# A PSUM bank for each group of the first transform, and odd rows tile by tile in turns

## The chip, the cores and the metric

The kernel runs on one core of a Trainium2 chip. The metric is the time of one execution on the device in microseconds (us). The engines of the core work beside each other, each through its own list of instructions in order: TensorE (PE, matrix products; PEld is its weight load), VectorE (DVE), ScalarE (ACT), GpSimd (POOL) and SyncE (SP), which here only issues DMAs. They wait for each other and for DMAs by semaphores. PE writes its products to PSUM, which has eight banks; DVE and ACT read them there.

## The reference

```python
x: (8, 3008, 256)                       # 8 sequences of 3008 rows
X = np.fft.fft(x, axis=1)
X = np.fft.fft(X, axis=2)
a = X.real.astype(np.float32).reshape(8 * 3008, 256)
h = a @ w_in                            # 256 -> 2048
r = np.maximum(h, 0.0)
out = (r * r) @ w_out                   # 2048 -> 256
```

All of it is float32.

## The kernel before

A two-dimensional Fourier transform whose real part is kept splits into cosine and sine products. For each sequence the kernel forms two tables in SBUF, P (`Pt`, from cosines along the rows) and Q (`Qt`, from sines), and a single row E (`Et`) for the middle column of the 256. E is the work of one row; in the first sequence it is carried through PE in the last, else unused, row of Q's products. Behind the transform follow the two layers: `front` multiplies P and Q with w_in, which has been multiplied with the second transform's tables (`G1`, `G2`), DVE joins the results (L637 to L640), ACT does relu and square (`combine`), and `back` multiplies with w_out. The output columns go in 6 blocks of up to 251, and each block in 8 steps `j` over the hidden dimension; `steps` is that list over all sequences.

The transforms of sequences 1 to 7 run spread between the steps of the sequence before (`between`). The transform of sequence 0 has nothing to hide behind: it is the prologue, and its order is written out by hand, in `pieces`, `groups` and the calls from `start()` to `spread_rest()`. The schedule is manual: on each engine the instructions stand in the order in which the program names them.

The prologue's parts are these.

- Seven row tiles of x are loaded (`load_x`). Tiles 0 to 3 belong to even rows (classes 0, 1, 2), tiles 4 to 6 to odd rows (class 3; `ODD0` is 4). `for_p(t)` folds tile t for P on DVE (L379, L395, L409) and ACT puts E's column into `lone` (L412, shown as `wsum`, whose memory it borrows; all its other columns are zero). `for_q(t)` folds it for Q (L383, L399, L409).
- Tables: `cosT` and `sinT`, loaded by SP (L183), first the cosines, then the odd tiles' sines, then win 1, then the even tiles' sines, then win 2 and further weights (L237).
- For P and for Q, and in each for two parities kp of the output column, there is a `group` of operations. `even_n` forms the even rows' products (L488) into one bank and ACT copies a part of them (`da`, L506). `join_4` and `join_2` combine the classes on DVE (L520/L524 for P, L515/L517 for Q). `odd_n` forms the odd rows' products. `join_1` combines both into `Pt`; for Q it comes as `join_lo` and `join_hi`.
- E: `even_e` and `odd_e` write E's products with `lone` (`wsum`) into a bank first, row 127 of the results, and Q's `even_n` and `odd_n` then add Q's 127 rows in the same banks.
- `begin_win(j)` starts to convert a part of w_in: two DVE operations split the number (L252, L257), ACT does three (L254, L255, L259), and `rounded(j)` the rest on DVE (L262, L264, L265). `win[j][1]` multiplies it with the second transform's tables (L280) and ACT copies the result to `G1`, `G2` (L281). `win[j][2]` forms one column for E (L289), and what it returns copies that to `gE` (L291).
- `awake(n)` issues n products of the identity matrix whose result nobody reads.
- `spread_e` spreads E's first 251 values over the partitions (L612, ACT L613); `spread_rest` does the rest through DRAM.

PSUM is shared out in three pools. `psd`, tag d, has two banks; `psh`, tag h, has two (the banks of `front`'s `ph`); `psm` has one bank each for mA, mB, mC, mD (the accumulators of `back`; mC and mD also take the products of L280). In the prologue before the change: `filled` (of `awake`) sits in mB; even rows of P take the two banks of d, one for each parity; even rows of E and Q take the same two banks after them; odd rows of P take the two h banks; odd rows of E and Q take mA for kp 0 and an h bank for kp 1; L289 of j = 0 takes mC, and `spread_e` a bank of d.

The numbers in `groups_at` count the list of operations: 0 to 4 are P's for kp 0 (even_n, join_4, join_2, odd_n, join_1), 5 to 9 the same for kp 1, 10 to 17 are Q's for kp 0 (even_n, join_4, join_2, odd_n, join_lo, even_e, odd_e, join_hi), and 18 to 25 those for kp 1.

Of the kernel before, what the change touches and what calls it, by code (L numbers as in the profile page):

```python
# [8 lines left out]
F32 = mybir.dt.float32  # L9
# [4 lines left out]
P = 128  # L14
# [68 lines left out]
def kernel(  # L83
# [13 lines left out]
    B, NROW, _, D = x.shape  # L97
# [7 lines left out]
    CH = 256  # L105
# [3 lines left out]
    NT = len(TILES)  # L109
# [16 lines left out]
    psh = ctx.enter_context(tc.tile_pool(name="psh", bufs=2, space=PSUM))  # L126
    psd = ctx.enter_context(tc.tile_pool(name="psd", bufs=2, space=PSUM))
    psm = ctx.enter_context(tc.tile_pool(name="psm", bufs=1, space=PSUM))
# [9 lines left out]
    ODD0 = NT - 3  # L138
# [60 lines left out]
    nc.vector.memset(ramp[:, 1:2], 255.0 * 2.0 ** 23)  # L199


    filled = psm.tile([P, CH], F32, name="filled", tag="mB")

    def awake(n):
        for _ in range(n):
            nc.tensor.matmul(filled[:, 0:P], ident, ident, start=True, stop=True)


    def pair_in(j):

        return moe_w_in.rearrange("(c p) (h j f) -> j c p h f", p=P, j=NJ, h=2)[j]
# [5 lines left out]
    def parts(w, k):  # L217
        return w.rearrange("p c (e h) -> p h (c e)", h=k)
# [22 lines left out]
    def convert(dst, raw):  # L241


        k = dst.shape[1]
        if raw.dtype == F32:
            return lambda: nc.vector.tensor_copy(dst, parts(raw[:, :, :, 0], k))
        low, high = raw[:, :, :, 0], raw[:, :, :, 1]
        m = scratch()
        e = fp.tile([P, 2, CH], F32, name="fd", tag="fd")
        mb, eb, rest = m.bitcast(U32), e.bitcast(U32), low.bitcast(F32)  # L250

        nc.vector.tensor_scalar(out=eb, in0=high, scalar1=20, scalar2=0x7FF,  # L252
                                op0=ALU.logical_shift_right, op1=ALU.bitwise_and)
        act(e, eb, AF.Relu, bias=ramp[:, 0:1], scale=-1.0)  # L254
        act(eb, e, AF.Relu, bias=ramp[:, 1:2], scale=-2.0 ** 23)  # L255

        nc.vector.tensor_scalar(out=mb, in0=high, scalar1=0xFFFFF, scalar2=0x100000,  # L257
                                op0=ALU.bitwise_and, op1=ALU.bitwise_or)
        act(rest, low, AF.Copy, scale=2.0 ** -32)  # L259

        def finish():
            nc.vector.scalar_tensor_tensor(out=eb, in0=high, scalar=0x80000000, in1=eb,  # L262
                                           op0=ALU.bitwise_and, op1=ALU.bitwise_or)
            tt(out=m, in0=mb, in1=rest, op=ALU.add)  # L264
            nc.vector.scalar_tensor_tensor(out=dst, in0=parts(m, k), scalar=2.0 ** -20, in1=parts(e, k),  # L265
                                           op0=ALU.mult, op1=ALU.mult)

        return finish


    def begin_win(j):

        w = ep.tile([P, 2, CH], F32, name="win", tag="sB" if j % 2 else "sA")
        finish = convert(parts(w, 1), win.pop(j, None) or load(pair_in(j)))

        def products():
            for tab, G, nm in ((cosd, G1, "mC"), (sind, G2, "mD")):
                pg = psm.tile([P, CH], F32, name="pg", tag=nm)
                for i in range(2):
                    nc.tensor.matmul(pg, tab[:, i], w[:, i], start=i == 0, stop=i == 1)  # L280
                nc.scalar.copy(G.rearrange("p (h j f) -> j p h f", h=2, j=NJ)[j],  # L281
                               pg.rearrange("p (h f) -> p h f", h=2))

        def for_e():

            ps = psd.tile([P, CH], F32, name="pe", tag="d") if j else psm.tile([P, CH], F32, name="pe", tag="mC")
            for h in range(2):
                fc = j + NJ * h
                nc.tensor.matmul(ps[:, h:h + 1], G2[:, fc * P:(fc + 1) * P], last, start=True, stop=True)  # L289

            return lambda: nc.vector.tensor_scalar_mul(gE[:, j::NJ], ps[:, 0:2], 0.5)  # L291

        win[j] = finish, products, for_e
# [42 lines left out]
    def columns(tab, t, part):  # L336

        nk, at = NC[0][3], PLACE[t]
        nq = (nk + 1) // 2
        return tab[:, 0, at + part * nq:at + (nk if part else nq)]  # L340
# [120 lines left out]
    def dft_ops(b):  # L461
# [7 lines left out]
        def group(kp, which):  # L469
            both_in = b == 0 and which == 1  # L470
            n = NE if b is None else P - 1 if which == 1 and b else P
            tab = sinT if which == 1 else cosT
            n2, _, n1, n0 = NC[kp]
            st = {}

            def product(ps, c, lone_e=False):

                ts = [t for t in range(NT) if TILES[t][0] == c]
                for t in ts:
                    rows = TILES[t][3]  # L480
                    if b is None:
                        w = we[0:rows, kp, t, 0:n]
                    elif lone_e:
                        w = lone[0:rows, 2 * t + kp]
                    else:
                        w = folded[b, t][0:rows, kp, PART[which]]
                        w = w if which else w[:, 0:n]
                    nc.tensor.matmul(ps[0:w.shape[-1]], w,  # L488
                                     (cosT if lone_e else tab)[0:rows, kp, PLACE[t]:PLACE[t] + NC[kp][c]],
                                     start=t == ts[0] and (lone_e or not both_in), stop=t == ts[-1] and not lone_e,  # L490
                                     skip_group_check=both_in)

            EVEN = ((0, 0, n2), (1, n2, n2), (2, 2 * n2, n1))

            def even_e():
                st["ps"] = psd.tile([P, 512], F32, name="pd", tag="d")
                for c, at, nk in EVEN:
                    product(st["ps"][:, at:at + nk], c, True)

# [33 lines left out]
                st["c"] = hp.tile([P, NC[0][3]], F32, name="dc2", tag="dc2", bufs=2)[0:n, 0:n0]  # L533
                both(st["c"][:, 0:n1], st["c"][:, n1:n0], a, ps[:, 2 * n2:2 * n2 + n1])

            def odd_tile():

                pool, tag = (psd, "d") if b != 0 else (psm, "mA") if kp == 0 and both_in else (psh, "h")
                ps = pool.tile([P, 512], F32, name="pd", tag=tag)[0:n]
                st["odd"] = ps[:, 0:n0]  # L540
                return ps

            def odd_e():
                product(odd_tile()[:, 0:n0], 3, True)

            def odd_n():
                if both_in:
                    return product(st["odd"], 3)
                ps = odd_tile()
                if not b:  # L550
                    return product(ps[:, 0:n0], 3)
                nq = (n0 + 2) // 2 if kp else (n0 + 1) // 2
                for part in range(2):
                    if kp:
                        tab, o = (cosT, sinT)[part], 0
                        to = ps[:, part * nq:part * nq + nq]
                        other = part != which
                    else:
                        tab, o = (cosT, sinT)[which], part
                        to = ps[:, part:n0:2]  # L560
                        other = part != which
                    for i, pair in enumerate(((ODD0, ODD0 + 1), (ODD0 + 2, NT))):
                        nc.tensor.matmul(to, folded[b, pair[other]][:, kp, PART[which]][:, 0:n],  # L563
                                         columns(tab, ODD0 + i, o), start=i == 0, stop=i == 1)
                if kp:
                    st["cos"] = hp.tile([P, nq], F32, name="oc", tag="oc", bufs=1)[0:n]
                    nc.scalar.copy(st["cos"], ps[:, 0:nq])
                    st["sin"] = ps[:, nq:2 * nq]
# [21 lines left out]
                both(dst[:, kp:kp + 2 * n0 - 1:2], dst[:, M - kp - 2 * (nh - 1):M - kp + 1:2], st["c"],  # L590
                     st["odd"], only)

            if both_in:
                return [(0.0, f) for f in (even_n, join_4, join_2, odd_n, join_lo, even_e, odd_e, join_hi)]
            ops = [(0.1, even_n), (0.4, join_4), (0.5, join_2), (0.1, odd_n), (0.8, join_1)]
            if b and kp:
                ops.insert(4, (0.5, join_odd))
# [179 lines left out]


    pieces = [fold(0, t) for t in range(NT)]
    start, *groups = [f for _, f in dft_ops(0)]  # L780

    def for_p(t):
        for i in (0, 2, 4):
            pieces[t][i]()

    def for_q(t):
        for i in (1, 3, 5):
            pieces[t][i]()

    def groups_at(*which):  # L790
        for i in which:
            groups[i]()

    def rounded(j):
        win[j][0]()
# [26 lines left out]
    win[0][1]()  # L822
    awake(2)
    for_p(3)
    groups_at(0, 5, 15, 23)
    for_q(1)
    for_p(4)
    for_p(5)
    for_q(2)
    for_p(6)  # L830
    groups_at(3, 8, 1, 2)
    for_q(4)
    groups_at(6, 7)
    for_q(5)
    groups_at(4, 16, 24)
    for_q(6)
    groups_at(13, 21, 9)
    copy_e = win[0][2]()
    begin_win(1)
    for_q(3)  # L840
    groups_at(10, 18)
    awake(14)
    rounded(1)
    begin_win(2)
    groups_at(11, 12, 14, 19, 20, 22)
    spread_e()
    groups_at(17, 25)
    copy_e()
    spread_rest()
    LAG = 2  # L850
# [39 lines left out]
    for i in range(len(steps) + LAG + 4):  # L890
        if i < len(steps):
            b, k0, n, j = steps[i]
# [96 lines left out]
```

## Time and profile before

| what | us |
|---|---|
| median of 5 runs (1949.26 to 1951.45) | 1949.78 |
| the profiled execution | 1949.47 |
| its span, first to last instruction | 1947.5 |
| PE busy (99% of the span) | 1933.3 |
| DVE busy (72%) | 1395.0 |
| ACT busy (47%) | 924.8 |
| POOL busy (60%) | 1173.8 |
| start of L612, the first product behind the prologue | 47.67 |

A line of the timeline gives start, length, engine, line, operation, out<-in, the shapes and the number of instructions; in brackets stands the idle time before it and what ended that. An f32 product is two records on PE. The chain that ended last is the work followed back from the end, at each step to what released it. PEclk, or "clock" in a table by stretches, is the TensorE clock that was granted, as a part of full speed; it was 0.996 in the mean.

### The profile page before, as it was taken

Reading aid. Unit: us, or ns where it says so; the run is one execution under the profiler, and the core shown is the slowest. Engines: PE = TensorE matmul, PEld = TensorE weight load, DVE = VectorE, ACT = ScalarE, POOL = GpSimd, SP = SyncE. Lnnn points to the kernel's source line nnn. Section 1 sums busy time; section 2 is a strip of 40 time slices with the busy share of each in tenths; the row PEclk is TensorE's granted clock in tenths of the full one; section 3 lists DMA queues with packets and bytes.
Section 4 is the critical chain, followed back from the end, with each engine's and each line's share of the span. In section 5 each row is a group of like instructions: output and inputs, shape, how many; then the busy total and the mean of one; then the engine's idle time right before and its main releaser. Section 6 shows DMA issues by size and latency. Waiting matters only on the chain.

```text
span 1947.5 us, 27716 instructions
## 1 busy us (share of the span) xinstructions
PE 1933.3 (99%) x9258; PEld 1718.9 (88%) x9258; DVE 1395.0 (72%) x3432; ACT 924.8 (47%) x1074; POOL 1173.8 (60%) x1708
## 2 busy tenths in 40 slices
PE   8999999999999999999999999999999999999998
PEld 7888888888988899888998889888898888988887
DVE  7998866777677766777667776677767777655554
ACT  2755544454444444544444454444544454444443
POOL 0047646676567665767566665666756676566655
PEclk8999999999999999999999999999999999999999
DMA  7342102111111101111011200121002101100101
GB/s 210 111 45 52 36 9 51 33 28 30 26 32 41 38 12 27 41 37 31 12 35 39 44 19 12 39 50 28 20 15 53 33 12 22 27 12 11 22 11 22
DMA packets 145562, 69.53 MB, mean 36 GB/s; under 512 B 129090, under 2 KB 136204, under 8 KB 145419
## 3 DMA queue, kind: packets, MB, share of 16 engines
q1 hardware_dynamic: 144960, 66.86, 15.9%
q8 instruction: 72, 1.18, 0.3%
q14 instruction: 71, 0.58, 0.1%
q0 software_dynamic: 176, 0.65, 0.1%
q10 hardware_dynamic: 283, 0.26, 0.0%
HBM read 43.03 MB, written 24.69 MB: 35 GB/s over the span
## 4 chain that ended last, share of the span: by engine, by line
PE 96%; DVE 3%; issue 0%; DMA 0%; ACT 0%; DVEq 0%
PE ph L635 16%; PE mC L687 16%; PE ph L634 16%; PE mA L687 16%; PE mB L687 16%; PE mD L687 8%; PE pd L488 3%; PE pd L563 2%; DVE m L264 0%; DVE fd L262 0%; DVE he L637 0%; PE mA L674 0%; PE mB L674 0%; DVE g L640 0%; DVE w L409 0%
## 5 line engine op out<-in xcount | busy, mean ns | idle before, releaser
L649 ACT ACTIVATE g<-g 128x1004 f32<-128x1004 f32 (+1 forms) x384 | 399.4, 1040 | 792.5 <-DVE g L640 459.1
L637 DVE SCALAR_TENSOR_TENSOR he<-Et,gE,ph 128x251 f32<-128x251 f32 (+1 forms) x768 | 362.1, 471 | 413.5 <-PE ph L635 411.2
L657 POOL TENSOR_TENSOR s<-g 128x251 f32<-128x251 f32 (+1 forms) x376 | 246.3, 655 | 658.8 <-ACT g L650 596.1
L634 PE MATMUL ph<-Pt,G 128*128 128x251 f32 (+1 forms) x1536 | 452.1, 375 | 0.0
L635 PE MATMUL ph<-Qt,G 127*128 127x251 f32 (+1 forms) x1536 | 451.8, 375 | 0.0
L650 ACT ACTIVATE g<-g 128x1004 f32<-128x1004 f32 (+1 forms) x384 | 399.3, 1040 | 12.1
L687 PE MATMUL mC<-s,wsum 128*128 128x251 f32 (+1 forms) x1504 | 381.7, 375 | 0.0
L687 PE MATMUL mA<-g,wout 128*128 128x251 f32 (+1 forms) x1504 | 379.8, 374 | 0.0
L639 DVE TENSOR_TENSOR g<-he,ph 128x251 f32<-128x251 f32 (+1 forms) x768 | 320.6, 417 | 55.3 <-POOL s L657 1.4
L635 PEld LDWEIGHTS ph<-Qt,G 127*128 127x128 f32 x1536 | 291.7, 190 | 36.1
L634 PEld LDWEIGHTS ph<-Pt,G 128*128 128x128 f32 x1536 | 288.0, 189 | 35.3 <-DVE g L640 0.8
L687 PEld LDWEIGHTS mC<-s,wsum 128*128 128x128 f32 x1504 | 285.7, 190 | 34.7
L687 PEld LDWEIGHTS mA<-g,wout 128*128 128x128 f32 x1504 | 282.9, 189 | 36.0 <-issue 1.3
L640 DVE TENSOR_TENSOR g<-he,ph 128x251 f32<-128x251 f32 (+1 forms) x768 | 314.3, 409 | 0.0
L659 POOL TENSOR_TENSOR s<-g 128x251 f32<-128x251 f32 (+1 forms) x376 | 305.5, 812 | 0.0
L658 POOL TENSOR_TENSOR s<-s,g 128x251 f32<-128x251 f32 (+1 forms) x376 | 274.5, 730 | 29.5
L660 POOL TENSOR_TENSOR s<-g,s 128x251 f32<-128x251 f32 (+1 forms) x376 | 253.7, 675 | 0.0
L687 PE MATMUL mB<-g,wsum 128*128 128x251 f32 (+1 forms) x752 | 220.5, 374 | 0.0
L687 PE MATMUL mD<-s,wout 128*128 128x251 f32 (+1 forms) x752 | 220.4, 374 | 0.0
L687 PE MATMUL mB<-s,wout 128*128 128x251 f32 (+1 forms) x752 | 219.9, 374 | 0.0
L687 PEld LDWEIGHTS mB<-g,wsum 128*128 128x128 f32 x752 | 142.6, 190 | 17.4
L687 PEld LDWEIGHTS mD<-s,wout 128*128 128x128 f32 x752 | 141.9, 189 | 17.7
(136 smaller groups left out, 1306.3 us busy)
## 6 DMA issues: line engine op xcount, KB each, us to landing
out_dram<-os SPq DMA_DIRECT2D x376, 56.0 KB
xt<-in_x_dram SPq DMA_DIRECT2D x32, 384.0 KB
xt<-in_x_dram SPq DMA_DIRECT2D x42, 128.0 KB
Et<-e_dram SPq DMA_DIRECT2D x7, 752.5 KB
xt<-in_x_dram SPq DMA_DIRECT2D x9, 512.0 KB
out_dram<-os SPq DMA_DIRECT2D x288, 6.8 KB
raw<-in_moe_w_in_dram SPq DMA_DIRECT2D x16, 256.0 KB
raw<-in_moe_w_out_dram SPq DMA_DIRECT2D x16, 256.0 KB
```

Of the source, the lines that this page charges most:

```text
L634: nc.tensor.matmul(hP, G1[:, fs], pt[:, ks], start=True, stop=True)
L635: nc.tensor.matmul(hQ, G2[0:P - 1, fs], qt[0:P - 1, ks], start=True, stop=True)
L637: nc.vector.scalar_tensor_tensor(out=t, in0=et[:, ks], scalar=gE[:, fc:fc + 1], in1=hP, op0=ALU.mult, op1=ALU.add)
L639: tt(out=g[:, h, 0, 0:n], in0=t, in1=hQ, op=ALU.add)
L640: tt(out=g[:, h, 1, 0:n][:, ::-1], in0=t, in1=hQ, op=ALU.subtract)
L649: act(v, v, AF.Relu)
L650: act(v, v, AF.Square)
L657: gt(out=s1, in0=g21, in1=g22, op=ALU.add)
L658: gt(out=s2, in0=s1, in1=g11, op=ALU.subtract)
L659: gt(out=s3, in0=g11, in1=g21, op=ALU.subtract)
L660: gt(out=s4, in0=g12, in1=s2, op=ALU.subtract)
L687: nc.tensor.matmul(acc[nm][:, i, 0:n], w, v[:, 0:n], start=j == 0 and i == 0, stop=j == NJ - 1, skip_group_check=True)
```

## The change

Only the prologue changes; the steps behind it are the same list of instructions on each engine.

- Banks. E's and Q's even rows get mC (kp 0) and mD (kp 1) instead of the two banks of d after P. E's and Q's odd rows get mA and mB. `filled` is taken from the two banks of d at each call of `awake`, and so is the tile of L289 for j = 0.
- The products of odd rows: instead of three tiles of one group after the other (P kp 0, P kp 1, E kp 0, E kp 1, Q kp 0, Q kp 1), the order is tile 4 of P for both parities, tile 4 of E for both, then tiles 5 and 6 in the same way, and behind them tile 4 of Q for both parities, tile 5, tile 6.
- DVE: the fold of tile 6 for Q comes ahead of P's two `join_1`, which stood on both sides of it.
- The second `awake` has 12 products instead of 14.

The diff, cut to its core; the renaming of group numbers to names is left out where the order stays.

```diff
-    filled = psm.tile([P, CH], F32, name="filled", tag="mB")
-
     def awake(n):
+        filled = psd.tile([P, CH], F32, name="filled", tag="d")
         for _ in range(n):
             nc.tensor.matmul(filled[:, 0:P], ident, ident, start=True, stop=True)
...
-            ps = psd.tile([P, CH], F32, name="pe", tag="d") if j else psm.tile([P, CH], F32, name="pe", tag="mC")
+            ps = psd.tile([P, CH], F32, name="pe", tag="d")
...
-            def product(ps, c, lone_e=False):
+            def product(ps, c, lone_e=False, only=None):
                 ts = [t for t in range(NT) if TILES[t][0] == c]
-                for t in ts:
+                for t in ts if only is None else ts[only:only + 1]:
...
             def even_e():
-                st["ps"] = psd.tile([P, 512], F32, name="pd", tag="d")
+                st["ps"] = psm.tile([P, 512], F32, name="pd", tag=("mC", "mD")[kp])
...
-            def odd_tile():
-                pool, tag = (psd, "d") if b != 0 else (psm, "mA") if kp == 0 and both_in else (psh, "h")
-                ps = pool.tile([P, 512], F32, name="pd", tag=tag)[0:n]
+            def odd_part(i, lone_e):
+                if i == 0 and lone_e == both_in:
+                    pool, tag = (psm, ("mA", "mB")[kp]) if both_in else (psh, "h")
+                    st["odd"] = pool.tile([P, 512], F32, name="pd", tag=tag)[:, 0:n0]
+                product(st["odd"], 3, lone_e, i)
...
     for_p(3)
-    groups_at(0, 5, 15, 23)
+    p_part("even")
+    q_part("even_e")
     for_q(1)
     for_p(4)
     for_p(5)
     for_q(2)
     for_p(6)
-    groups_at(3, 8, 1, 2)
+    for i in range(NT - ODD0):
+        p_part(f"odd{i}")
+        q_part(f"odd_e{i}")
+    groups[0, 0, "join_4"]()
+    groups[0, 0, "join_2"]()
     for_q(4)
-    groups_at(6, 7)
+    groups[0, 1, "join_4"]()
+    groups[0, 1, "join_2"]()
     for_q(5)
-    groups_at(4, 16, 24)
     for_q(6)
-    groups_at(13, 21, 9)
+    p_part("join_1")
+    q_part(*(f"odd{i}" for i in range(NT - ODD0)))
     copy_e = win[0][2]()
     begin_win(1)
     for_q(3)
-    groups_at(10, 18)
-    awake(14)
+    q_part("even")
+    awake(12)
     rounded(1)
     begin_win(2)
-    groups_at(11, 12, 14, 19, 20, 22)
+    for kp in range(2):
+        for nm in ("join_4", "join_2", "lo"):
+            groups[1, kp, nm]()
     spread_e()
-    groups_at(17, 25)
+    q_part("hi")
     copy_e()
```

`p_part(name)` and `q_part(name)` call the named operation of P or of Q for kp 0 and then for kp 1.

More of the change, by code (lines that the diff above doesn't have):

```diff
@@ L534, in join_2, with odd_n @@
                 both(st["c"][:, 0:n1], st["c"][:, n1:n0], a, ps[:, 2 * n2:2 * n2 + n1])
-            def odd_tile():
-                pool, tag = (psd, "d") if b != 0 else (psm, "mA") if kp == 0 and both_in else (psh, "h")
-                ps = pool.tile([P, 512], F32, name="pd", tag=tag)[0:n]
-                st["odd"] = ps[:, 0:n0]
[L541 to L550, printed above, removed]
+            def odd_part(i, lone_e):
[3 more added lines that the diff above has]
+                product(st["odd"], 3, lone_e, i)
+            def odd_n():
+                ps = psd.tile([P, 512], F32, name="pd", tag="d")[0:n]
+                st["odd"] = ps[:, 0:n0]
+                if b is None:
                     return product(ps[:, 0:n0], 3)
@@ L591, in join_1 @@
                      st["odd"], only)
-            if both_in:
-                return [(0.0, f) for f in (even_n, join_4, join_2, odd_n, join_lo, even_e, odd_e, join_hi)]
+            if b == 0:
+                named = [("even", even_n), ("join_4", join_4), ("join_2", join_2), ("lo", join_lo), ("hi", join_hi),
+                         ("join_1", join_1), ("even_e", even_e)]
+                for i in range(NT - ODD0):
+                    named += [(("odd", "odd_e")[e] + str(i), lambda i=i, e=e: odd_part(i, e == 1)) for e in range(2)]
+                return [((which, kp, nm), f) for nm, f in named]
             ops = [(0.1, even_n), (0.4, join_4), (0.5, join_2), (0.1, odd_n), (0.8, join_1)]
@@ L779 @@
     pieces = [fold(0, t) for t in range(NT)]
-    start, *groups = [f for _, f in dft_ops(0)]
+    (_, start), *groups = dft_ops(0)
+    groups = dict(groups)
     def for_p(t):
@@ L788, in for_q, with p_part, q_part @@
             pieces[t][i]()
-    def groups_at(*which):
-        for i in which:
-            groups[i]()
+    def p_part(*names):
+        for nm in names:
+            for kp in range(2):
+                groups[0, kp, nm]()
+    def q_part(*names):
+        for nm in names:
+            for kp in range(2):
+                groups[1, kp, nm]()
     def rounded(j):
@@ L830 @@
     for_p(6)
-    groups_at(3, 8, 1, 2)
+    for i in range(NT - ODD0):
+        p_part(f"odd{i}")
+        q_part(f"odd_e{i}")
+    groups[0, 0, "join_4"]()
+    groups[0, 0, "join_2"]()
     for_q(4)
-    groups_at(6, 7)
+    groups[0, 1, "join_4"]()
+    groups[0, 1, "join_2"]()
     for_q(5)
-    groups_at(4, 16, 24)
     for_q(6)
-    groups_at(13, 21, 9)
+    p_part("join_1")
+    q_part(*(f"odd{i}" for i in range(NT - ODD0)))
     copy_e = win[0][2]()
@@ L840 @@
     for_q(3)
-    groups_at(10, 18)
-    awake(14)
+    q_part("even")
+    awake(12)
     rounded(1)
     begin_win(2)
-    groups_at(11, 12, 14, 19, 20, 22)
+    for kp in range(2):
+        for nm in ("join_4", "join_2", "lo"):
+            groups[1, kp, nm]()
     spread_e()
-    groups_at(17, 25)
+    q_part("hi")
     copy_e()
```

## The prediction

> **What bounds the kernel now.** I read the page first: TensorE (PE) holds 96% of the chain that ended last and is busy 99% of the span, so only PE's idle time and its slow stretches can be won. The list of waits, PE alone, says where the idle time is:
>
> ```profile
> engine line waited for: us in total, times, longest us
> PE pd L488 <- DVE dc L524: 4.2, 1, 4.2
> PE pe L289 <- ACT G L281: 2.7, 2, 2.3
> ...
> PE mA L674 <- DVE wout L265: 0.5, 1, 0.5
> ```
>
> All of it lies before 100 us. So I read PE's timeline there (start, length, line, out<-in, number of records; a product is two records):
>
> ```profile
> 17.31 2.89 PE L488 MATMUL pd<-cosT,w 95*128 95x95 f32 x16
> 24.36 5.00 PE L488 MATMUL pd<-cosT,wsum 95*128 95x95 f32 x16 [4.16 <-DVE dc L524]
> 29.16 5.11 PE L488 MATMUL pd<-cosT,w 128*128 128x377 f32 x12
> 34.11 3.97 PE L488 MATMUL pd<-cosT,wsum 128*128 128x377 f32 x12
> 37.91 3.97 PE L488 MATMUL pd<-sinT,w 128*127 128x377 f32 x12
> 41.72 0.50 PE L289 MATMUL pe<-ident,G 128*128 128x1 f32 x4
> 42.08 2.42 PE L488 MATMUL pd<-sinT,w 95*127 95x95 f32 x16
> 44.34 3.29 PE L206 MATMUL filled<-ident 128*128 128x128 f32 x28
> 47.67 0.66 PE L612 MATMUL pe<-Qt,ident 128*128 128x251 f32 x2
> ```
>
> The reader sees E's even rows wait 4.16 us for P's joins on VectorE (DVE), which free their bank, and then take 5.00 us where the equal group at 42.08 takes 2.42. The table by stretches gives the reason, the granted clock (PE busy, clock, DMA share, GB/s):
>
> ```profile
> 17.80:21.20 3.40, 2.29 (x13) 1.00 1.02 280
> 21.20:24.60 3.40, 0.24 (x1) 0.50 1.08 296
> 24.60:28.00 3.40, 3.30 (x13) 0.50 1.05 262
> 28.00:31.40 3.40, 3.40 (x9) 0.50 0.49 96
> ...
> 55.40:58.80 3.40, 1.15 (x7) 1.00 0.00 0
> 58.80:62.20 3.40, 3.40 (x11) 0.50 0.48 154
> ```
>
> Half clock follows stretches in which PE was busy 2.29 and 1.15 of 3.4 us, and holds 10.2 us the first time. Last, the chain in order of time: from 49.27 it is DVE's nearly alone, until PE takes over for good:
>
> ```profile
> 49.27 0.49 DVE he L637
> ...
> 98.96 0.70 DVE wout L265
> 99.70 0.69 PE mA L674 x2
> ```
>
> So what counts is when step 0's first DVE operation starts (49.27). Behind 99.70 PE has no wait but 0.5 us in the last store, and a shift reaches the end whole.
>
> **The change, part by part.** *E's even rows get banks mC and mD.* Their last users, two ACT copies of G, end by 17.4, so the 4.16 us go: these products start at about 20.1, where P's even rows end. PE is then busy on through 17.8 to 21.2, with gaps of about 0.3 us; the stretches at 41.7 and 51.9, as full, kept clock 1.00, so I expect no drop at 21.2. The group then takes 2.26 (42.08 to 44.34) and not 4.80 (24.36 to 29.16), and ends at 22.4.
>
> *Odd rows of P and E in turns.* The same 36 records, each with its own weight load before and after. At full clock twelve take 3.80 (34.11 to 37.91), the first twelve took 4.95; so the odd rows end at 22.4+3x3.80 = 33.8, not 41.72: 8.0 us earlier (4.16 wait, 2.54 and 1.15 clock, 0.1 rounding). The turns let PE start with what is there. The trace holds each transfer's landing: the three odd cosine tiles land at 21.3, 22.6, 24.3 and are wanted at 22.4, 24.9, 27.4; the odd sine tiles at 26.2, 28.1, 29.7, wanted at 30.0, 31.2, 32.5. DVE's folds for them end at 23.2 (P) and, below, 29.9 (Q). Nothing stalls; the price of the turns is nil, covered by these 0.5 to 4 us.
>
> *Even rows of Q.* L289 takes 0.36, so they could start at 34.1. Their last sine piece lands at 35.04: the first parity's last tile runs 35.1 to 35.4, the second parity ends at 36.5. About 1 us of the 8.0 is lost here.
>
> *DVE's queue.* Tile 6's Q fold (1.58, from 33.33) moves ahead of P's first join, into the 4.05 us that DVE idles before 32.41: 28.3 to 29.9. P's odd rows end on PE at 28.7, so both joins (0.92 each, L520 and L524) run to 31.7; the next win's two splitting operations (0.67; its data landed at 31.0) to 32.4, tile 3's fold (1.57) to 34.0, the rounding (1.93) to 35.9. Next stand two operations on win 2, whose second half lands at 36.60. DVE is strictly in order here, so Q's joins, queued behind, wait too: they start at 36.65+0.67 = 37.3. ACT's copy for them is ready 0.63 after the last tile's second record (43.09 to 43.72 now), at 35.9, so the transfer is last. Now they start at 43.72: 6.4 us gained. SP issues the same list in the same order; a load there waits for the landing eight places before it, and buffer releases come no later, so I leave the landings where they are.
>
> *Smaller parts.* Filling matmuls 14 to 12: 12x0.224 (3.13/14, 44.34 to 47.47) = 2.7, so PE ends at 39.2; L612 needs Q's low joins, 3.95 after their start (43.72 to 47.67), at 41.25. That leaves a new idle of 2.05 us. L289's tile, the filling and L612 now share two banks; L612 gets the filling's bank, not the one that L291 still has to read, so no wait is added. P's odd rows take the ph banks, free until step 0.
>
> *The new idle and the clock.* The nearest rows are 1.15 busy of 3.4 (drop) and gaps of 0.3 to 0.5 (none). The drops and rises in the table stand 3.4 apart on one grid; where that falls in another run isn't known. If the idle falls inside one stretch, L612 and step 0's eight records run at half speed: the first L635 is 0.85 later, the second 1.7 more, of which DVE's 1.17 per half hides part: 1.4, with L612 1.8. Bounds 0 to 1.8; I take 0.8. The Trainium skill, "TensorE: Matmul & The Clock Gate", section "HAM oscillation", warns of idle gaps above some 3.4 us only; by it the sum would be 6.4 without the 0.8 (1943.4), but in this trace 2.25 us was enough.
>
> Sum: -6.4+0.8 = -5.6. From step 0 on DVE's work is unchanged up to 99.70, where PE had waited 0.54 for it. PE's own chain follows, since its wait at 58.61 is set by DVE and ACT; the half clock at 58.8 may move, but costs PE 1.7 off the chain. The profiled run took 1949.47 (span 1947.5 and 2.0 around it), so 1943.9; the median is 0.3 above it: **1944.2 us**.
>
> **The rivals.** *A, the cover is thinner.* The gain is capped by data (win 2 later by 2 to 3 us), or the clock still drops at 21.2 and holds two stretches of 3.4, moving PE 3.4 later and the joins to 39.3. For it: DMA share is 1.0 until 28 us. Against: the landings follow from one list. Gain 2 to 3.9: 1945.9 to 1947.8.
>
> *B, slower.* One mechanism: the gate does not see products in turns as busy and holds half clock from 21.2 through the P and E turns. Even rows left over cost 1.1 more, 24 odd records 7.6 more, the twelve of Q 0 to 3.8: odd rows end at 42.5 to 46.3. It decides once PE loses over 8.0 us, since then the joins start after 43.72: +0.8 to +4.6, 1950.6 to 1954.4. For it: 24.6 to 28.0, all with the mostly zero wsum, was busy 3.30 and kept 0.50. Against: 34.11 to 37.91, twelve wsum records, ran at 1.00. The same skill page, section "A second HAM failure mode: psum-queue depth-cycling", speaks against this change: cycling banks can make the gate swing; it would give these times. In this trace the rows from 64.26 on (L674) swap banks mA and mB product by product at clock 1.00, so the measurement stands against it.
>
> *C, it does nothing:* the banks are still taken and the 4.16 us appear under another name. Against: mC and mD are free at 17.4. 1949.8.
>
> **How the numbers follow.** Forecast 78% (1942.5 to 1945.9), A 14%, C 3%, B 5%. The lower bound: win 2 landing earlier frees the joins at 36.6 (-7.1) with no clock loss, 1942.7, less 0.2 of scatter. The upper: half of A, 1946.8. 0.2% (3.9 us) is what a measurement can tell here. Faster is the forecast, 0.78; same A and C, 0.17; slower B, 0.05.
>
> **What would show it.** In the changed profile: no wait at wsum products; clock 1.00 from 21 to 38; L289 near 33.8; Q's joins (L515) start near 37.3, behind win 2's L251; L612 near 41.3 with about 2 us idle before it; half clock behind that or not; first L637 42.9 to 44.3. Wrong: L515 started by ACT or PE, or a clock of 0.5 inside the turns.

## The result and the profile after

The changed kernel takes 1944.71 us in the median of 25 runs (1943.31 to 1950.0), against 1950.15 in 45 runs (1949.06 to 1951.69) of the kernel before. The ratio is 0.9977 with a 95% interval of 0.9971 to 0.9982, or 3.5 to 5.7 us less. One thing stands out beside the gain: the runs before lie within 2.6 us, those after within 6.7.

The profiled execution of the changed kernel took 1947.47, more than its median, so it shows how the slower executions come about. Its list of waits, PE alone:

```profile
engine line waited for: us in total, times, longest us
PE pd L487 <- DMA cosT<-in_cos_s_dram: 3.3, 1, 3.3
PE pe L288 <- ACT G L280: 2.7, 2, 2.2
...
PE pe L612 <- DVE Qt L515: 0.5, 1, 0.5
```

The 4.2 us for P's joins are gone. A wait of 3.3 us stands in the list that was not there before: the same products of even rows (L487, L488 before) now wait for cosine tiles. PE's timeline of that execution shows where:

```profile
16.19 0.58 PE L487 MATMUL pd<-cosT,w 95*128 95x95 f32 x4
20.05 3.71 PE L487 MATMUL pd<-cosT,w 96*128 96x189 f32 x12 [3.28 <-DMA cosT<-in_cos_s_dram]
23.55 4.43 PE L487 MATMUL pd<-cosT,wsum 95*128 95x95 f32 x16
27.77 2.10 PE L487 MATMUL pd<-cosT,w 128*128 128x377 f32 x4
29.71 1.43 PE L487 MATMUL pd<-cosT,wsum 128*128 128x377 f32 x4
...
39.83 0.50 PE L288 MATMUL pe<-ident,G 128*128 128x1 f32 x4
...
45.78 0.66 PE L612 MATMUL pe<-Qt,ident 128*128 128x251 f32 x2 [0.49 <-DVE Qt L515]
```

The wait is inside P's even rows, between class 1 and class 2, whose last transfer landed at 20.4 us here and at 18.4 in the profile before. E's even rows follow P's without a pause, as the new banks allow, but take 4.43 us and not the 2.3 that they need at full clock. The table by stretches (PE busy, clock, DMA share, GB/s) says why:

```profile
17.80:21.20 3.40, 1.15 (x4) 0.66 0.99 253
21.20:24.60 3.40, 3.40 (x15) 0.50 1.07 266
24.60:28.00 3.40, 3.40 (x13) 0.50 1.09 267
28.00:31.40 3.40, 3.40 (x10) 0.84 0.93 207
```

The clock fell at 18.9 us and stayed at 0.50 for 10.2 us. L612, the first product behind the prologue, starts at 45.78 instead of 47.67: of 8.0 us on PE 1.9 are left in this execution. From L612 to the end of the span it is 1899.9 us here and 1899.8 before, so all that the change does is done by then. Q's joins start late, and ACT's copy of PE's products releases them, not win 2:

```profile
41.84 0.32 DVE L515 SCALAR_TENSOR_TENSOR db<-pd,signs,da 128x95 f32<-128x95 f32 x1 [0.74 <-ACT da L506]
```

### The profile page after: what moved, and what is told of

Same layout as the page of the kernel before. It is cut to its first block, busy times and chain, and to the rows that moved or that the text cites. A ratio compares the mean times of both kernels' runs of the same rounds, so it can differ in the third digit from the quotient of the medians.

```text
span 1945.7 us, 27713 instructions
## 1 busy us (share of the span) xinstructions
PE 1931.1 (99%) x9254; PEld 1717.4 (88%) x9254; DVE 1394.9 (72%) x3432; ACT 924.9 (48%) x1074; POOL 1174.3 (60%) x1708
## 3 DMA queue, kind: packets, MB, share of 16 engines
q8 instruction: 72, 1.18, 0.3%
## 4 chain that ended last, share of the span: by engine, by line
PE 96%; DVE 3%; DMA 1%; issue 0%; SPq 0%; ACT 0%; DVEq 0%
PE ph L635 16%; PE ph L634 16%; PE mC L687 16%; PE mA L687 16%; PE mB L687 16%; PE mD L687 8%; PE pd L487 3%; PE pd L559 2%; DMA xt<-in_x_dram 0%; DVE m L263 0%; DVE fd L261 0%; DMA cosT<-in_cos_s_dram 0%; DVE he L637 0%; PE mA L674 0%; PE mB L674 0%
## 5 line engine op out<-in xcount | busy, mean ns | idle before, releaser
L637 DVE SCALAR_TENSOR_TENSOR he<-Et,gE,ph 128x251 f32<-128x251 f32 (+1 forms) x768 | 362.1, 472 | 413.8 <-PE ph L635 411.4
```

The lines of the kernel that those rows point to most:

```text
L637: nc.vector.scalar_tensor_tensor(out=t, in0=et[:, ks], scalar=gE[:, fc:fc + 1], in1=hP, op0=ALU.mult, op1=ALU.add)
```

## The experiments

Each kernel ran beside the kernel before. Ratios are to that.

| kernel | median us | lowest to highest | runs | ratio (95%) |
|---|---|---|---|---|
| changed kernel again | 1946.58 | 1943.94 to 1947.71 | 10 | 0.9977 (0.9968 to 0.9986) |
| banks alone | 1943.89 | 1943.23 to 1947.85 | 6 | 0.9969 (0.9958 to 0.9981) |
| turns alone | 1950.46 | 1949.39 to 1951.29 | 11 | 0.9999 (0.999 to 1.0008) |
| class 2 cosines issued first | 1946.24 | 1944.37 to 1949.22 | 11 | 0.9979 (0.9971 to 0.9988) |
| 14 filling products first | 1945.3 | 1943.71 to 1946.46 | 7 | 0.997 (0.9959 to 0.9982) |
| banks alone, 14 filling | 1944.57 | 1943.8 to 1946.19 | 8 | 0.9969 (0.9959 to 0.998) |
| win 2 behind the high joins | 1947.01 | 1942.19 to 1949.21 | 10 | 0.9979 (0.997 to 0.9988) |
| changed kernel, third time | 1946.96 | 1945.04 to 1948.65 | 11 | 0.9981 (0.9972 to 0.999) |
| 14 filling, win 2 behind | 1943.49 | 1942.98 to 1944.39 | 5 | 0.9965 (0.9952 to 0.9979) |
| banks alone, 14 filling, win 2 behind | 1945.04 | 1944.03 to 1947.26 | 9 | 0.9974 (0.9964 to 0.9984) |
| even rows in two halves, and both | 1942.35 | 1941.69 to 1944.52 | 5 | 0.996 (0.9947 to 0.9973) |
| the same again | 1942.41 | 1942.0 to 1944.17 | 5 | 0.996 (0.9948 to 0.9973) |

The first four ran on one occasion with 27 runs of the kernel before (median 1950.48), the next three and the first run of the halves on a second (18 runs, 1950.47), the rest on a third (19 runs, 1950.47).

### The changed kernel again, twice

No edit.

> The changed kernel once more. Theory 1 (cover): its time is set by when the cosine tiles of class 2 land. If they land before about 18.5 us, PE goes from P's even rows straight on, the clock stays 1.00 from 21 to 38 us and the run takes 1943 to 1945 us; if they land after 20 us, PE idles some 3 us before them, the clock is 0.50 for about 10 us and the run takes 1946 to 1950. Theory 2 (new idle): the spread comes from the idle time before L612 and the clock behind it; then runs with late tiles are not slower than others.

> The changed kernel a third time, beside the next three. Theory 1 (cover): two groups of runs, 1943.3 to 1945.7 where the clock held or fell late, 1946 to 1950 where it fell at about 19 us; median 1944.5 to 1946.7.

With the first occasion this makes 47 executions, each with its mean granted clock. The 18 whose clock was 0.996 or lower took 1946.69 to 1950.0; the 29 with 0.997 or more took 1943.31 to 1947.51, all but three of them under 1946.3. So there is a lower and an upper group, and the mean clock tells them apart nearly, not wholly: it counts half clock anywhere in the execution. The three profiles have the same 10.2 us of it in the prologue; the second and the third have 3.4 us more near 57 us, which does not show in the time behind L612, and a mean of 0.996 where the first has 0.997. The profiles show the way into the upper group. First the changed kernel the second time, then the third:

```profile
16.26 0.58 PE L487 MATMUL pd<-cosT,w 95*128 95x95 f32 x4
18.17 3.50 PE L487 MATMUL pd<-cosT,w 96*128 96x189 f32 x12 [1.33 <-DMA cosT<-in_cos_s_dram]
21.46 4.43 PE L487 MATMUL pd<-cosT,wsum 95*128 95x95 f32 x16
```

```profile
19.07 3.21 PE L487 MATMUL pd<-cosT,w 96*128 96x189 f32 x12 [1.56 <-DMA cosT<-in_cos_s_dram]
22.08 4.43 PE L487 MATMUL pd<-cosT,wsum 95*128 95x95 f32 x16
```

Idle times of 1.33 and 1.56 us were enough for the clock to fall, at 19.0 and 20.2, each time for 10.2 us; L612 starts at 44.81 and 45.70. The reader is to see that the clock costs more than the wait. From the start of P's even rows to L288 PE took 23.64, 22.59 and 22.82 us in the three profiles, of which 3.28, 1.33 and 1.56 are the wait; with win 2 moved (below), where the clock held, it took 16.79 with a wait of 0.51. Without the waits that is 20.36, 21.26 and 21.26 against 16.28: half clock costs 4.1 to 5.0 us. The expectation had a landing after 20 for the drop and one before 18.5 for none. The two landed between, at 18.7 and 19.6, and fell: the bound lies lower than I put it. Theory 2 does not explain the upper group: in all three profiles the idle time before L612 is only 0.5 us and L612 itself runs at full clock (0.66 us). The median of the third group, 1946.96, is above the 1946.7 expected. No execution of the changed kernel itself was profiled with the clock held; its schedule then is seen below, with win 2 moved.

In the third profile the span is 1.2 us longer behind L612 than in the others; its last product is where it should be, and only the last store's issue on SP takes longer (2.42 us instead of 1.18).

### Banks alone

```diff
-    filled = psm.tile([P, CH], F32, name="filled", tag="mB")
     def awake(n):
+        filled = psd.tile([P, CH], F32, name="filled", tag="d")
...
-            ps = psd.tile([P, CH], F32, name="pe", tag="d") if j else psm.tile([P, CH], F32, name="pe", tag="mC")
+            ps = psd.tile([P, CH], F32, name="pe", tag="d")
...
-                st["ps"] = psd.tile([P, 512], F32, name="pd", tag="d")
+                st["ps"] = psm.tile([P, 512], F32, name="pd", tag=("mC", "mD")[kp])
...
-                pool, tag = (psd, "d") if b != 0 else (psm, "mA") if kp == 0 and both_in else (psh, "h")
+                pool, tag = (psd, "d") if b != 0 else (psm, ("mA", "mB")[kp]) if both_in else (psh, "h")
```

> The new banks, with the order of products, of VectorE's folds and the 14 filling products as before the change. Theory 1 (cover): the 4.2 us wait of E's even rows goes, as in the changed kernel; but P's third odd tile is wanted at about 23.7 us and lands at 24.3 to 27.3, so PE waits 0.6 to 3.6 us there: 1945 to 1949 us. Rival (the banks are all of it): no wait there that matters, the same time as the changed kernel, 1944.7 within 0.7. Rival (the turns carry the gain): as before the change, 1949 to 1951.

1943.89 in six runs, beside 1946.58 for the changed kernel in the same group of runs, with intervals that overlap. That is the rival "the banks are all of it" as far as the gain goes; below the changed kernel by more than the 0.7 that it allowed, though no difference between the two is shown. Theory 1's 1945 to 1949 missed the median. In two of the six runs, both 1943.89, the mean clock was 1.0: the gain is there without the turns. The profile is that of the slowest run, 1947.85; in it PE's wait was again for class 2 (3.18 us), the clock fell behind it for 6.8 us, and P's odd rows, slowed by that, found all three tiles there: nothing for the turns to win.

### Turns alone

```diff
             def even_e():
-                st["ps"] = psm.tile([P, 512], F32, name="pd", tag=("mC", "mD")[kp])
+                st["ps"] = psd.tile([P, 512], F32, name="pd", tag="d")
...
-    def awake(n):
-        filled = psd.tile([P, CH], F32, name="filled", tag="d")
+    def awake(n, tag="mB"):
+        filled = psm.tile([P, CH], F32, name="filled", tag=tag)
```

(The second filling sits in mD, L288's tile in mC.)

> The turns of odd rows and the order of folds of the changed kernel, with E's even rows in the two banks of P's even rows as before the change. Theory 1 (cover): the wait of about 4.2 us for P's joins and the half clock behind it stay, 1949 to 1951 us. Rival (the turns carry the gain): under 1947. Rival (turns cost something in themselves): over 1951.

No gain, 0.9999 (0.999 to 1.0008). The profile shows what can keep the kernel before so steady:

```profile
19.75 3.71 PE L487 MATMUL pd<-cosT,w 96*128 96x189 f32 x12 [3.00 <-DMA cosT<-in_cos_s_dram]
25.05 5.00 PE L487 MATMUL pd<-cosT,wsum 95*128 95x95 f32 x16 [1.59 <-DVE dc L524]
```

Here class 2 landed at 20.1 and PE waited 3.00 us for it; the wait for the joins is then 1.59 instead of 4.16. The joins set the start of E's rows in either case, so with this late tile they start only 0.69 us later than in the profile before (25.05 against 24.36). The wait that the change removes had been the cover of this other one.

### Class 2 cosines issued first

```diff
+    load_table(cosT, cos_s, (2, 3))
     load_x(0, 4)
     load_x(0, 5)
-    load_table(cosT, cos_s, (2, 3))
```

> The changed kernel with the four transfers of class 2 cosines issued ahead of row tiles 4 and 5. Theory 1 (cover): PE's wait before P's even rows goes in every run, clock 1.00 from 21 us on, VectorE waits up to 1.5 us for tile 4 instead; median 1943 to 1944.7 and few runs over 1946. Theory 2 (new idle): median and spread of the changed kernel, 1943.3 to 1950.

This missed: 1946.24, no better than the changed kernel. The wait moved on to the first odd tile:

```profile
16.96 2.34 PE L487 MATMUL pd<-cosT,w 95*128 95x95 f32 x16
19.14 2.34 PE L487 MATMUL pd<-cosT,wsum 95*128 95x95 f32 x16
27.28 2.85 PE L487 MATMUL pd<-cosT,w 128*128 128x377 f32 x4 [5.80 <-DMA cosT<-in_cos_s_dram]
```

Both groups of even rows ran at full clock, 2.34 each; then PE had nothing to do until 27.1, when the first odd cosine tile landed, and the clock fell at 25.6. The profile is that of its slowest run, 1949.22. Class 2 had landed at 17.5, but that odd tile came later than in any other profile (21.0 to 25.2), so whether the new order itself delayed it is not shown; what is shown is that PE, once past class 2, ran ahead of the transfers.

### Fourteen filling products first

```diff
-    awake(2)
+    awake(14)
     for_p(3)
```

> The changed kernel with 14 filling products, not 2, ahead of P's even rows. Theory 1 (cover): they bridge PE's wait for the cosine tiles of class 2, so the clock stays 1.00 from 17 to 38 us; PE's even rows start at 20 to 20.5 us in every run, L612 at 42 to 43.5, and the time is narrow, 1943.5 to 1945, with no run over 1946. Rival (the late landing itself is the loss, the clock is none of it): the same median and spread as the changed kernel (1944.7 to 1946.6; 1943.3 to 1950).

The upper group is gone: 1943.71 to 1946.46, where the changed kernel itself reached 1950.0. Class 2 landed as late as in the profile of the changed kernel (20.4), yet PE filled the time, and the clock stayed at 1.00 to 43.5. "The clock is none of it" falls by the clock and the spread; the median alone, 1945.3, would fit it as well. The expectation was too narrow: four of the seven runs are above 1945, the highest above 1946. What then comes last is the prediction's: VectorE's queue of this execution,

```profile
38.83 0.43 DVE L251 TENSOR_SCALAR fd<-raw 128x512 uint32<-128x512 uint32 x1 [1.49 <-DMA raw<-in_moe_w_in_dram]
39.17 0.42 DVE L256 TENSOR_SCALAR m<-raw 128x512 uint32<-128x512 uint32 x1
39.50 0.31 DVE L515 SCALAR_TENSOR_TENSOR db<-pd,signs,da 128x95 f32<-128x95 f32 x1
...
46.39 0.48 DVE L637 SCALAR_TENSOR_TENSOR he<-Et,gE,ph 128x251 f32<-128x251 f32 x1 [1.99 <-PE ph L635]
```

Win 2 landed at 38.7, VectorE waited 1.49 us for it and Q's joins had to queue behind. So did PE, and the idle time ahead of L612 cost what was feared:

```profile
38.33 2.84 PE L205 MATMUL filled<-ident 128*128 128x128 f32 x24
43.45 1.17 PE L612 MATMUL pe<-Qt,ident 128*128 128x251 f32 x2 [2.28 <-DVE Qt L515]
44.41 1.05 PE L634 MATMUL ph<-Pt,G 128*128 128x251 f32 x2
```

2.28 us idle, then half clock from 43.5 for 3.4 us; VectorE's first L637 comes 2.94 us after L612 (46.39-43.45) where it is 1.61 in the changed kernel (47.39-45.78), and from L612 to the end it is 1901.3 instead of 1899.9: 1.3 to 1.4 us lost. This is the profile of the slowest of its seven runs.

### Banks alone with the same filling

The filling is the edit above on the kernel with banks alone.

> The new banks without the turns, with 14 filling products ahead of P's even rows instead of 2. If the turns are of use at full clock, P's third odd tile is wanted at about 26 us and lands at 24 to 27.5, so PE waits up to 1.5 us and the time is up to 1.5 us above that of the same filling with turns; if they are of no use, both times agree within 0.7.

1944.57 against 1945.3, within the scatter of both. PE did wait for the third odd tile, 1.12 us, as expected of a kernel without turns, but win 2 held Q's joins in either kernel (VectorE waited 1.24 us for it here), so the wait cost nothing.

### Win 2 behind the high joins

```diff
     rounded(1)
-    begin_win(2)
     for kp in range(2):
...
     q_part("hi")
+    begin_win(2)
     copy_e()
```

> The changed kernel with the two splitting operations on win 2 moved from ahead of Q's joins to behind the high joins. Theory 1 as in the prediction (win 2's landing is the last thing Q's joins wait for where the clock holds): the fast end of the runs moves from 1943.3 down to 1942 to 1943, and runs with a dropped clock, in which PE's products are last, stay at 1946 to 1948. Rival (PE's products are last in all runs): no change of the fast end, and up to 0.7 more where VectorE has no idle time to take the moved operations.

The fast end moved as the first expectation said, to 1942.19 and 1942.63, though with two runs only; the other eight, with clocks of 0.995 to 0.998, are at 1946.21 to 1949.21 where 1946 to 1948 were expected. The profile is one of the two, and it is the only one of a kernel without added filling in which the clock held:

```profile
17.88 2.29 PE L487 MATMUL pd<-cosT,w 96*128 96x189 f32 x12 [0.51 <-DMA cosT<-in_cos_s_dram]
20.01 2.34 PE L487 MATMUL pd<-cosT,wsum 95*128 95x95 f32 x16
22.19 1.43 PE L487 MATMUL pd<-cosT,w 128*128 128x377 f32 x4
...
29.78 3.96 PE L487 MATMUL pd<-sinT,w 128*127 128x377 f32 x12
33.58 0.50 PE L288 MATMUL pe<-ident,G 128*128 128x1 f32 x4
```

```profile
17.80:21.20 3.40, 3.23 (x22) 1.00 1.03 281
21.20:24.60 3.40, 3.40 (x17) 1.00 1.09 289
```

Class 2 landed at 18.4, as in the profile before; PE idled 0.51 us, and the clock did not fall. This is the schedule of the prediction, to 0.3 us: E's rows at 20.01 (20.1), odd rows at 22.19 (22.4) to 33.58 (33.8).

### Clock and win 2 together, with and without turns

Both edits, on the changed kernel and on the one with banks alone.

> The changed kernel with 14 filling products ahead of P's even rows and win 2's two operations behind the high joins. Theory 1 (cover): the clock holds in all runs and win 2 no longer holds Q's joins; PE's products are last: even rows at 19.5 to 20.5 us, Q's joins 17.4 us later, L612 at 41 to 42: 1942.5 to 1944, without the upper group. Rival (clock and win 2 are not the two causes): still two groups, or the 1943.7 to 1946.5 of the filling alone.

> The same two edits on the kernel with new banks and without the turns. With win 2 out of the way and the clock held PE's products are last, so the turns must show: without them PE waits 0 to 1.5 us for the third odd cosine tile, and the median is 0.3 to 1.5 us above the kernel with turns. If the turns are of no use even here, both agree within 0.5.

With turns 1942.98 to 1944.39: no upper group, and under the filling alone. Without turns 1945.04, 1.55 us above, just past the 1.5 that was expected, and the profile, of the slowest of its nine runs (1947.26), has the waits:

```profile
25.83 0.87 PE L487 MATMUL pd<-cosT,w 128*128 128x377 f32 x2 [0.80 <-DMA cosT<-in_cos_s_dram]
27.54 4.46 PE L487 MATMUL pd<-cosT,w 120*128 120x377 f32 x8 [0.84 <-DMA cosT<-in_cos_s_dram]
31.84 3.97 PE L487 MATMUL pd<-cosT,wsum 128*128 128x377 f32 x12
```

The clock fell behind these waits, at 0.50 from 27.8 to 31.2 us: the eight records at 27.54 take 4.46 us, where the same eight took 2.77 in the banks alone with filling (26.92). The cost here is the waits and again the clock; with the turns P's odd rows had neither. So the turns are of use once PE comes last; no run shows a use before. The two intervals overlap (0.9952 to 0.9979 and 0.9964 to 0.9984); the runs hardly do.

### Even rows in two halves: a version that beats both

On top of win 2's move: classes 0 and 1 of P and E for both parities first, six filling products in an h bank, then class 2 of all four groups; 14 filling products ahead of L612.

```diff
-    p_part("even")
-    q_part("even_e")
+    p_part("even_p0")
+    q_part("even_e0")
+    awake(6, psh, "h")
+    p_part("even_p1")
+    q_part("even_e1")
...
-    awake(12)
+    awake(14)
```

> A version meant to beat both: the changed kernel with win 2's two operations behind the high joins, even rows of P and E in two halves (classes 0 and 1 of all four groups first, then 6 filling products, then class 2), and 14 filling products ahead of L612. Theory 1 (cover): PE has work or filling until 19.8 us and the clock holds unless class 2 lands after 21; Q's joins start at about 36.5 us, L612 at 40.5 to 41.5: 1942 to 1943.5. Rival (transfers bound the prologue whatever the order): 1944 or more.

> The version with even rows in two halves, fillings and win 2's operations behind the high joins, again: median 1942 to 1943, at least 2 us under the changed kernel of the same call, no run over 1945.

1942.35 and 1942.41, ratios 0.996 (0.9947 to 0.9973 and 0.9948 to 0.9973), 8.1 us below the kernel before. Beside it on the third occasion the changed kernel took 1946.96 in its 11 runs, and the slowest run here (1944.17) is under the fastest there (1945.04). On the second occasion the highest was 1944.52; none passed 1945. Useful products now stand where PE had to wait. What each of the edits adds is not separated: beside the filling and win 2's move with turns (1943.49) the halves are 1.1 us lower, and the intervals overlap. The second profile:

```profile
17.06 1.03 PE L487 MATMUL pd<-cosT,w 95*128 95x95 f32 x8
17.93 1.06 PE L487 MATMUL pd<-cosT,wsum 95*128 95x95 f32 x8
18.82 1.53 PE L205 MATMUL filled<-ident 128*128 128x128 f32 x12
20.19 1.45 PE L487 MATMUL pd<-cosT,w 96*128 96x189 f32 x8
```

PE has no wait between 14 us and L612 (its L624, at 40.12), and Q's joins follow VectorE's own work without one.

## Why the prediction was right, and where not

- *The median and the sign.* 1944.71 lies in the range and 0.5 us from the forecast; the ratio makes it 4.5 us faster, the medians 5.4, where 5.6 were said. There is luck in this. The sum adds up a schedule with the clock held, and its number is that of the lower group only; 15 of the first 26 executions lie in 1942.5 to 1945.9, the span that was given 78%, and 7 of the 21 later ones. The two later medians, 1946.58 and 1946.96, lie above it.
- *The banks.* Right: the 4.16 us wait went, and banks alone carry the gain.
- *"I expect no drop at 21.2."* This is the step that failed, for the upper group. It rested on one execution, whose class 2 tiles landed at 18.4, and on "I leave the landings where they are". In the other profiles with this order of transfers they land at 18.0 to 21.5. While E's rows waited for the joins this was hidden; without that wait, in all three profiles of the changed kernel, PE idles 1.3 to 3.3 us inside P's even rows, and half clock for 10.2 us costs 4.1 to 5.0 us: 6.3 to 7.4 together, nearly the 7.85 of wait and half clock (4.16, 2.54 and 1.15) that the prediction took off. Both signs that the prediction named for being wrong stand there, L515 started by ACT and a clock of 0.5 inside the turns. Rival A named this, the clock falling and holding, at 14%: at 21.2 us for two stretches, joins at 39.3; it was at 18.9 to 20.2 for three, and the joins started at 40.9 to 41.8. Its price was 1945.9 to 1947.8; the 18 executions with the lowest clock took 1946.7 to 1950.0.
- *The turns.* "Price nil" is right: 24 records in 7.59 us (22.19 to 29.78) with win 2 moved, 7.6 in the prediction. What they win was not stated; no run shows any gain in the changed kernel itself, and 1.55 us between medians once filling and win 2's move make PE the last.
- *Win 2 ahead of Q's joins.* Right where the clock holds, as VectorE's 1.49 us wait shows. In the profiles of the changed kernel PE was last instead. The landing itself, 36.60 in the sum, was not fixed either: win 2's second half came at 36.9 to 41.2 in the other profiles.
- *The new idle.* 2.05 us said; 2.28 with the filling, 1.00 with win 2 moved, 0.5 where the clock had fallen. Its cost was taken at 0.8 with bounds 0 to 1.8; the one profile that shows it has 1.3 to 1.4.
- *Behind step 0.* Right. From L612 to the end of the span eleven of the fourteen profiles lie between 1899.8 and 1900.2, whether half clock stood at some 57 us or not; it is off the chain, as said. The exceptions are the third run of the changed kernel (1901.2, its last transfers), the filling (1901.3, step 0 at half clock) and win 2 moved (1900.6, half clock for 6.8 us from 50.8).
- *Rival B*, half clock throughout the turns because of them, fell: with win 2 moved they run at 1.00 from start to end. *Rival C* fell with the wait list, where the 4.16 us are gone, and with the time.

Why the same transfers land up to 3.5 us apart from one execution to another was not tried and stays open. So does whether banks alone are really faster than the changed kernel.

## What to carry to other kernels

A wait that is removed may have covered another one that no list shows; before counting the gain, look at what else that product waits for and how far its arrival varies over several executions, not in one. Here a short idle time of PE ahead of a long run of products cost more through the clock (4.1 to 5.0 us) than by itself (1.3 to 3.3); a few products that nobody needs, or useful ones moved up, were cheap cover. And once one bound is gone, the next in the queue, here a load that VectorE waits for in order, decides what a finer order of products is worth.

## What the runs showed of the hardware

- The clock fell after idle times of 1.33 and 1.56 us, and after 0.80 and 0.84 close together (banks alone, filling, win 2 behind); it held after 0.51, after 1.00 (win 2 moved, before L612) and after 1.12 (banks alone, filling). The length alone does not decide: the wait of 2.25 us in step 0 was followed by a fall in the second and third profiles of the changed kernel and not in the first (54.47 to 56.72). Each stretch of half clock in the first 70 us of a profile lasted 3.4 us or two to four times that (6.8, 10.2, 13.7). The Trainium skill ("TensorE: Matmul & The Clock Gate", section "HAM oscillation") warns of gaps above about 3.4 us; these runs differ, and they decide.
- Once down it stayed at 0.50 through stretches in which PE was busy 3.40 of 3.40 us with products of 95 to 189 columns (21.2 to 28.0 in the changed kernel), 10.2 us in all. In step 0 of the kernel with filling, with 251 columns, it came back after 3.4 us, but with win 2 moved only after 6.8 (50.8 to 57.7). Whether the size of the products makes the difference was not tried by itself and stays open.
